# Attention and two gated layers on one core: the 896 tokens cut as 480 + 416 columns, not 448 + 448

## The chip, the core and the metric

The kernel runs on one core of a Trainium2 chip. The metric is the device time of one execution in microseconds (us), lower is better. The runs below are separate executions of the whole kernel. One of them was recorded by the hardware profiler, and the rows shown are of that one.

## The reference

Inputs are q, k, v of shape 2 x 12 x 448 x 64, and float64 weights. The attention is causal; its output is laid out as 896 tokens (2 batches of 448) by 768 channels. Two layers follow:

```python
x = attention(q, k, v)            # 896 x 768, float32
g = x @ w_gate                    # 768 x 1536
v = x @ w_val                     # 768 x 1536
y = (g * sigmoid(g) * v) @ w_out  # 1536 x 768
h = y @ w_in2                     # 768 x 2048
out = relu(h) ** 2 @ w_out2       # 2048 x 768
```

## The kernel before

After the attention (the first 95 us or so) all activations lie with their channels on the 128 partitions and the 896 tokens along the free dimension, in tiles of 128 x 896. Every number, of activations and weights alike, is kept as two parts, hi and lo, in the type float32r, and each product is made of three: hi by hi, lo by hi, hi by lo.

A *unit* of weights is 128 x 768 numbers. There are 68: 12 pairs of gate and value (`g`, `v`), 12 of the way down (`o`, two for each of six output blocks `y`), 16 of the second way up (`h`), and 16 of the second way down (`f`). A unit comes in as 768 KB of float64 on SP's queue and is turned into a hi and a lo tile by nine instructions of DVE and ACT (`split_w`, lines 366 to 394), which run two units ahead of TensorE.

In the three stages before the last, a block of 128 output channels has two PSUM banks, one for the tokens of each batch (`halves(b)`: columns 0 to 447 and 448 to 895). `mm3` (lines 615 to 623) issues six matmuls for each block of 128 input channels: the weights are the stationary operand (128 x 128), the activations the moving one (448 columns). The order is hi weights by hi activations for bank 0 and bank 1, hi by lo for both, lo by hi for both. A pair of matmuls here means those two, which share their weights and differ in bank. A unit of gate, value or second way up has 6 x 6 = 36 matmuls, and so has one of the way down:

```python
        for b in bs:
            nc.tensor.matmul(out=pss[b][:, :S], lhsT=hi, rhs=mhi[:, halves(b)], start=first, stop=False)
```

The very first unit (gate, m = 0) has its bank 0 done ahead, inside the attention (`early_mm`, 448 columns).

When a block is complete, its two banks are read and turned into the next stage's tiles. These steps are put into the list `later` and are taken from it one at a time, between the steps of the weights' splitting (`follow_up`). For gate and value they are a sigmoid on ACT (L707), multiplications on DVE (L711), a copy to hi on ACT (L715) and the rest to lo on POOL (L716); for the way down a copy (L748) and a subtraction (L752); for the second way up Relu, Square and a copy on ACT (L772 to L775) and a subtraction on DVE (L779). Each of these handles one bank, 448 columns.

The last stage has the roles turned round: activations are stationary (128 tokens), weights move, 384 columns at a time (`add_up`, line 793).

The pool of PSUM has all 8 banks, taken in turn.

Of the kernel before, what the change touches and what calls it, by code (L numbers as in the profile page):

```python
# [265 lines left out]
def tile_attention_moe_moe(ctx, tc, q, k, v, w_gate, w_val, w_out, w_in2, w_out2, out):  # L266
# [22 lines left out]
    def bank(name):  # L289
        t = ps_p.tile([128, 512], F32, tag="b", name=name)  # L290
        keep_warm(t, idle["n"])
        idle["n"] = 0
        return t
# [139 lines left out]
    def unit(kind, m, j):  # L433
        n = units.index((kind, m, j))
        split_to(n + 2)
        load_w(n + 5)
        return split_t[n]
# [8 lines left out]
    def halves(b):  # L446
        return slice(b * S, (b + 1) * S)


    att = ExitStack()  # L450
    raw_p = att.enter_context(tc.tile_pool(name="qkvraw", bufs=2))
# [160 lines left out]
            op=ALU.subtract)  # L612


    def mm3(pss, hi, lo, mhi, mlo, first, last):

        bs = list(pss)
        for b in bs:
            nc.tensor.matmul(out=pss[b][:, :S], lhsT=hi, rhs=mhi[:, halves(b)], start=first, stop=False)  # L619
        for b in bs:  # L620
            nc.tensor.matmul(out=pss[b][:, :S], lhsT=hi, rhs=mlo[:, halves(b)], start=False, stop=False)  # L621
        for b in bs:
            nc.tensor.matmul(out=pss[b][:, :S], lhsT=lo, rhs=mhi[:, halves(b)], start=False, stop=last)  # L623

    def gate_or_val(kind, m, bs):
        hi, lo = unit(kind, m, 0)
        pss = {b: bank(kind) for b in bs}
        for kk in range(KD):
            c = slice(kk * 128, (kk + 1) * 128)
            mm3(pss, hi[:, c], lo[:, c], x_hi[kk], x_lo[kk], kk == 0, kk == KD - 1)  # L630
        return pss

    def emit_fixed():

# [18 lines left out]
            state["split"] += 1  # L653

    def early_mm(n, kk):
        hi, lo = split_t[n]
        if kk == 0:
            early[n] = bank("early")
        c = slice(kk * 128, (kk + 1) * 128)
        mm3({0: early[n]}, hi[:, c], lo[:, c], x_hi[kk], x_lo[kk], kk == 0, kk == KD - 1)  # L660

    def early_out(n):
        t = early_p.tile([128, S], F32, tag=f"e{n}", name="early")
# [10 lines left out]
    with tc.manual_schedule():  # L674
        nc.vector.memset(warm, 0.0)
        keep_warm(bank("idle"), 7)
        emit_consts()
        emit_fixed()
        free = 4000
        for start, cost, engine, key in attention_plan(NP, NPAIR, NC, S, U, KD).run():  # L680
            if key[0] == "Q":
                continue
            if engine == "PE":
                if start < Warmth.FROM:
                    idle["n"] = max(0, int((start - free) / (430 if start < 6800 else 215)))
                free = start + cost
            work[key[0]](*key[1:])
            idle["n"] = 0
        att.close()

        ay_p = ctx.enter_context(tc.tile_pool(name="ay", bufs=1))
        tmp_p = ctx.enter_context(tc.tile_pool(name="tmp", bufs=2))
        extra = [act_tile(ay_p, f"b{i}") for i in range(32)]


        g_hi = [extra[2 * m] for m in range(KF1)]
        g_lo = [extra[2 * m + 1] for m in range(KF1)]

        sg, up = {}, {}

        def sigmoids(ps):
            for z in range(B):
                sigmoid(ps[z], z)

        def sigmoid(ps, z):
            sg[z] = tmp_p.tile([128, S], F32, tag="sg", name="sg")
            nc.scalar.activation(out=sg[z], in_=ps[:, :S], func=AF.Sigmoid)  # L707

        def times(o, ps, z):
            o[z] = o.get(z) or tmp_p.tile([128, S], F32, tag="u", name="u")  # L710
            nc.vector.tensor_tensor(out=o[z], in0=ps[:, :S], in1=sg[z], op=ALU.mult)  # L711

        def gated(m, z):
            hs, u = halves(z), up.pop(z)
            nc.scalar.activation(out=g_hi[m][:, hs], in_=u, func=AF.Copy)  # L715
            nc.gpsimd.tensor_tensor(  # L716
                out=g_lo[m][:, hs], in0=u, in1=g_hi[m][:, hs].bitcast(F32), op=ALU.subtract)

        n = 0
        for m in range(KF1):  # L720
            for kind in "gv":
                ps = gate_or_val(kind, m, [1] if n < NEARLY else [0, 1])
                if n < NEARLY:
                    ps[0] = early[n]
                n += 1
                if kind == "g":
                    later += [partial(sigmoids, ps), *(partial(times, sg, ps[z], z) for z in range(B))]
                else:
                    later.append(lambda: None)
                    for z in range(B):  # L730
                        later += [partial(times, up, ps[z], z), partial(gated, m, z)]


        y_hi = extra[24:30]
        y_lo = extra[30:32] + x_hi[:4]
        for m in range(KD):
            pss = {b: bank("y") for b in range(B)}
            for j in range(2):
                hi, lo = unit("o", m, j)
                n = KF1 // 2  # L740
                for kk in range(n):
                    c = slice(kk * 128, (kk + 1) * 128)
                    f = j * n + kk
                    mm3(pss, hi[:, c], lo[:, c], g_hi[f], g_lo[f], f == 0, f == KF1 - 1)

            def first_part(m, pss):
                for b in range(B):
                    nc.scalar.activation(out=y_hi[m][:, halves(b)], in_=pss[b][:, :S], func=AF.Copy)  # L748

            def rest(m, pss, b):  # L750
                hs = halves(b)
                nc.vector.tensor_tensor(  # L752
                    out=y_lo[m][:, hs], in0=pss[b][:, :S], in1=y_hi[m][:, hs].bitcast(F32),
                    op=ALU.subtract)

            later += [partial(first_part, m, pss), partial(rest, m, pss, 0), partial(rest, m, pss, 1)]


        free = x_hi[4:] + x_lo + extra[:24]
        r_hi, r_lo = free[0:32:2], free[1:32:2]  # L760
        for m in range(KF2):
            hi, lo = unit("h", m, 0)
            pss = {b: bank("h") for b in range(B)}
            for kk in range(KD):
                c = slice(kk * 128, (kk + 1) * 128)
                mm3(pss, hi[:, c], lo[:, c], y_hi[kk], y_lo[kk], kk == 0, kk == KD - 1)
            u = {}

            def squares(m, pss, u):
                for b in range(B):  # L770
                    r = tmp_p.tile([128, S], F32, tag="sg", name="r")
                    nc.scalar.activation(out=r, in_=pss[b][:, :S], func=AF.Relu)  # L772
                    u[b] = tmp_p.tile([128, S], F32, tag="u", name="r2")
                    nc.scalar.activation(out=u[b], in_=r, func=AF.Square)
                    nc.scalar.activation(out=r_hi[m][:, halves(b)], in_=u[b], func=AF.Copy)  # L775

            def rest(m, u, b):
                hs = halves(b)
                nc.vector.tensor_tensor(  # L779
                    out=r_lo[m][:, hs], in0=u[b], in1=r_hi[m][:, hs].bitcast(F32), op=ALU.subtract)  # L780

            later += [partial(squares, m, pss, u), partial(rest, m, u, 0), partial(rest, m, u, 1)]


        N = DM // 2
        NTK = NT // 128
        for half in range(2):
            pss = [bank("o") for _ in range(NTK)]
            def add_up(hi, lo, u, z, t):
                f = 2 * u + z  # L790
                c, tk = slice(z * N, (z + 1) * N), slice(t * 128, (t + 1) * 128)
                for n, (a, w) in enumerate(((r_hi, hi), (r_hi, lo), (r_lo, hi))):
                    nc.tensor.matmul(  # L793
                        out=pss[t][:, :N], lhsT=a[f][:, tk], rhs=w[:, c], start=f + n == 0,
                        stop=f == KF2 - 1 and n == 2)

            for u in range(FU):
                hi, lo = unit("f", half, u)
                order = [(z, t) for z in range(2) for t in range(NTK)]
                if u == FU - 1:  # L800

                    order.sort(key=lambda x: x[1])
                for z, t in order:
                    add_up(hi, lo, u, z, t)
            for t in range(NTK):
                o = tmp_p.tile([128, N], F32, tag="osb", name="osb", bufs=6)
                if t % 2:
                    nc.vector.tensor_copy(out=o, in_=pss[t][:, :N])
                else:
                    nc.scalar.activation(out=o, in_=pss[t][:, :N], func=AF.Copy)  # L810
                nc.sync.dma_start(
                    out=out[t * 128:(t + 1) * 128, half * N:(half + 1) * N], in_=o)
# [30 lines left out]
```

## Time and profile before

| | |
|---|---|
| time, median of 3 runs | 598.9 us (598.78 to 600.12) |
| the profiled execution, first to last instruction | 598.2 us |
| TensorE busy | 592.2 us, 99% |
| VectorE (DVE) busy | 475.2 us, 79% |
| ScalarE (ACT) busy | 282.7 us, 47% |
| GpSimd (POOL) busy | 86.7 us, 14% |
| DMA, mean rate | 109 GB/s |

The profiled execution's own time is known by its span alone, 598.2 us; the median of the runs is 0.7 us longer. A matmul's recorded duration runs beyond the start of the next one, since matmuls are pipelined, so the spacing of the starts tells what a matmul costs in a row of them, not its duration.

### The profile page before, as it was taken

How to read it: one execution, taken by the hardware profiler on the slowest of the kernel's cores; microseconds unless marked ns; L12 is line 12 of the kernel's file. 1: busy time of each engine (PE TensorE's matmuls, PEld its weight loads, DVE VectorE, ACT ScalarE, POOL GpSimd, SP SyncE). 2: the span in 40 equal slices, each digit the busy share in tenths (PEclk: the TensorE clock that was granted, in tenths of full speed). 3: DMA queues.
4: the chain of work that ended last, by engine and by line, in shares of the span. 5: the costliest groups of instructions: out<-in, count | busy, mean ns of one | idle time of the engine just before them, and what ended most of it. 6: DMA issues, size and time to landing. Idle time of an engine off the chain costs nothing.

```text
span 598.2 us, 8837 instructions
## 1 busy us (share of the span) xinstructions
PE 592.2 (99%) x3256; PEld 530.8 (89%) x3257; DVE 475.2 (79%) x839; ACT 282.7 (47%) x555; POOL 86.7 (14%) x154
## 2 busy tenths in 40 slices
PE   8999999999999999999999999999999999999997
PEld 5777778999999999999999999999999999999997
DVE  4789977999999999998877777888888887649741
ACT  6999984333333333333222225666666642222201
POOL 4576770211111111111000000000000000000000
PEclk9999999999999999999999999999999999999999
DMA  8784402333333333333333332333333344345202
GB/s 169 166 220 95 122 2 85 108 109 112 108 110 109 105 106 106 106 105 107 121 107 102 106 109 91 107 107 105 106 105 107 105 112 153 106 142 136 80 1 93
DMA packets 80779, 65.06 MB, mean 109 GB/s; under 512 B 34912, under 2 KB 76640, under 8 KB 80736
## 3 DMA queue, kind: packets, MB, share of 16 engines
q1 hardware_dynamic: 79808, 64.27, 36.6%
q8 instruction: 26, 0.43, 0.3%
q10 hardware_dynamic: 928, 0.23, 0.2%
q14 instruction: 17, 0.14, 0.1%
HBM read 61.73 MB, written 2.75 MB: 108 GB/s over the span
## 4 chain that ended last, share of the span: by engine, by line
PE 95%; DVE 2%; POOL 1%; issue 1%; ACT 1%; DMA 1%; SPq 0%; POOLq 0%; ACTq 0%
PE o L793 19%; PE h L621 7%; PE h L619 7%; PE h L623 7%; PE y L619 5%; PE v L623 5%; PE v L619 5%; PE y L623 5%; PE y L621 5%; PE v L621 5%; PE g L623 5%; PE g L619 5%; PE g L621 5%; PE s L520 4%; PE x L598 3%; PE pt L576 2%
## 5 line engine op out<-in xcount | busy, mean ns | idle before, releaser
L381 ACT ACTIVATE whi<-wa 128x768 fp32r<-128x768 f32 x68 | 57.6, 847 | 179.3 <-DVE wa L378 136.8
L793 PE MATMUL o<-whi,b 128*128 128x384 f32 x336 | 85.6, 334 | 0.0
L369 DVE TENSOR_SCALAR wa<-wa 128x768 f32<-128x768 f32 x68 | 41.4, 608 | 43.5 <-ACT wa L366 43.5
L378 DVE SCALAR_TENSOR_TENSOR wa<-wraw,wa 128x768 uint32<-128x768 uint32 x68 | 75.2, 1106 | 0.0
L366 ACT ACTIVATE wa<-wraw 128x768 f32<-128x768 f32 x68 | 61.6, 905 | 17.6 <-DVE wlo L394 17.6
L394 DVE TENSOR_TENSOR wlo<-wa,wr 128x768 fp32r<-128x768 f32 x68 | 65.7, 967 | 0.1
L388 DVE SCALAR_TENSOR_TENSOR wr<-wraw,wr 128x768 f32<-128x768 uint32 x68 | 65.0, 955 | 0.1
L391 DVE TENSOR_TENSOR wa<-wa,whi 128x768 f32<-128x768 f32 x68 | 64.6, 950 | 0.4 <-ACT whi L381 0.4
L793 PEld LDWEIGHTS o<-whi,b 128*128 128x128 f32 x336 | 60.8, 188 | 0.0
L793 PE MATMUL o<-wlo,b 128*128 128x384 f32 x168 | 56.1, 334 | 0.0
L623 PE MATMUL h<-b,wlo 128*128 128x448 f32 x192 | 55.2, 368 | 0.0
L619 PE MATMUL h<-b,whi 128*128 128x448 f32 x192 | 55.1, 368 | 0.0
L716 POOL TENSOR_TENSOR b<-u,b 128x448 fp32r<-128x448 f32 x24 | 29.0, 1209 | 159.4 <-ACT b L715 159.4
L541 ACT ACTIVATE P<-P,st 128x448 f32<-128x448 f32 (+2 forms) x96 | 47.7, 503 | 3.3 <-DVE st L535 1.9
L559 POOL TENSOR_SCALAR P<-P,st 128x448 f32<-128x448 f32 (+1 forms) x88 | 45.1, 531 | 10.2 <-DVE st L551 5.3
L535 DVE CUSTOM_DVE_ANT_0 P<-s,mask 128x448 f32<-128x448 f32 (+2 forms) x96 | 34.8, 412 | 11.9 <-PE s L520 10.5
L619 PE MATMUL v<-ahi,whi 128*128 128x448 f32 x144 | 41.4, 368 | 0.0
L619 PE MATMUL y<-b,whi 128*128 128x448 f32 x144 | 41.4, 368 | 0.0
L621 PE MATMUL y<-b,whi 128*128 128x448 f32 x144 | 41.4, 368 | 0.0
L623 PE MATMUL v<-ahi,wlo 128*128 128x448 f32 x144 | 41.4, 368 | 0.0
L621 PE MATMUL v<-alo,whi 128*128 128x448 f32 x144 | 41.4, 368 | 0.0
L623 PE MATMUL y<-b,wlo 128*128 128x448 f32 x144 | 41.3, 368 | 0.0
(96 smaller groups left out, 1145.1 us busy)
## 6 DMA issues: line engine op xcount, KB each, us to landing
wraw<-in_moe_w_out_dram SPq DMA_DIRECT2D x28, 768.0 KB, 4.4
wraw<-in_moe_w_in_dram SPq DMA_DIRECT2D x16, 768.0 KB, 4.6
wraw<-in_moe_w_gate_dram SPq DMA_DIRECT2D x12, 768.0 KB, 4.3
wraw<-in_moe_w_val_dram SPq DMA_DIRECT2D x12, 768.0 KB, 4.3
raw<-in_q_dram SPq DMA_DIRECT2D x24, 112.0 KB, 2.7
out_dram<-osb SPq DMA_DIRECT2D x14, 192.0 KB, 1.9
raw<-in_k_dram SPq DMA_DIRECT2D x22, 112.0 KB, 2.8
v<-in_v_dram SPq DMA_DIRECT2D x24, 96.0 KB, 2.7
```

What stands on the lines that cost most here:

```text
L366: nc.scalar.activation(out=af, in_=high.bitcast(F32), func=AF.Abs)
L378: nc.vector.scalar_tensor_tensor(out=a, in0=high, scalar=0xC0000000, in1=a, op0=ALU.bitwise_and, op1=ALU.bitwise_or)
L381: nc.scalar.activation(out=split_t[n][0], in_=af, func=AF.Copy)
L388: nc.vector.scalar_tensor_tensor(out=rf, in0=low, scalar=2.0 ** -52, in1=rf, op0=ALU.mult, op1=ALU.mult)
L391: nc.vector.tensor_tensor(out=af, in0=af, in1=split_t[n][0].bitcast(F32), op=ALU.subtract)
L394: nc.vector.tensor_tensor(out=split_t[n][1], in0=af, in1=r[0].bitcast(F32), op=ALU.add)
L541: nc.scalar.activation(out=a, in_=a, func=AF.Exp, scale=-1.0, bias=st(0), accum_out=st(1))
L559: (nc.vector if n_on_dve(h) else nc.gpsimd).tensor_scalar(out=o, in0=a, scalar1=st(2), scalar2=1.0, op0=ALU.mult, op1=ALU.mult)
L619: nc.tensor.matmul(out=pss[b][:, :S], lhsT=hi, rhs=mhi[:, halves(b)], start=first, stop=False)
L621: nc.tensor.matmul(out=pss[b][:, :S], lhsT=hi, rhs=mlo[:, halves(b)], start=False, stop=False)
L623: nc.tensor.matmul(out=pss[b][:, :S], lhsT=lo, rhs=mhi[:, halves(b)], start=False, stop=last)
L793: nc.tensor.matmul(out=pss[t][:, :N], lhsT=a[f][:, tk], rhs=w[:, c], start=f + n == 0, stop=f == KF2 - 1 and n == 2)
```

## The change

The second bank no longer begins at the second batch. In gate and value (all but the first pair of units), in the way down and in the second way up, bank 0 takes columns 0 to 479 and bank 1 columns 480 to 895. The first pair of units keeps 448 + 448, since its early bank is made so. The number of matmuls, their order, the weights that they load and the reading of the banks stay; the instructions that read the banks take 480 and 416 columns in place of 448 and 448, and the four buffers of the pool `tmp` become 480 columns wide. `mm3` and `gate_or_val` become one helper, `products`. The attention and the last stage are not touched.

```diff
+    HALVES = (0, S), (S, S)
+    CUTS = (0, 480), (480, 416)
+
+    def at(cut):
+        return slice(cut[0], cut[0] + cut[1])
...
-    def mm3(pss, hi, lo, mhi, mlo, first, last):
-
-        bs = list(pss)
-        for b in bs:
-            nc.tensor.matmul(out=pss[b][:, :S], lhsT=hi, rhs=mhi[:, halves(b)], start=first, stop=False)
...
+    def products(pss, cuts, w, xs, first, last):
+
+        n = len(xs)
+        zs = list(pss)
+        for k, p, z in [(k, p, z) for k in range(n) for p in range(3) for z in zs]:
+            at, cols = cuts[z]
+            c = slice(k * 128, (k + 1) * 128)
+            nc.tensor.matmul(
+                out=pss[z][:, :cols], lhsT=w[p == 2][:, c], rhs=xs[k][p == 1][:, at:at + cols],
+                start=first and k == 0 and p == 0, stop=last and k == n - 1 and p == 2)
...
+        def times(o, ps, z, c):
+            o[z] = o.get(z) or tmp_p.tile([128, W], F32, tag="u", name="u")
+            nc.vector.tensor_tensor(
+                out=o[z][:, :c[1]], in0=ps[:, :c[1]], in1=sg[z][:, :c[1]], op=ALU.mult)
...
+        W = max(c[1] for c in CUTS)
+        x_parts = list(zip(x_hi, x_lo))
         n = 0
         for m in range(KF1):
+            cuts = CUTS if m else HALVES
             for kind in "gv":
-                ps = gate_or_val(kind, m, [1] if n < NEARLY else [0, 1])
+                w = unit(kind, m, 0)
+                ps = {z: bank(kind) for z in range(n < NEARLY, B)}
+                products(ps, cuts, w, x_parts, True, True)
...
             for j in range(2):
-                hi, lo = unit("o", m, j)
-                n = KF1 // 2
-                for kk in range(n):
-                    c = slice(kk * 128, (kk + 1) * 128)
-                    f = j * n + kk
-                    mm3(pss, hi[:, c], lo[:, c], g_hi[f], g_lo[f], f == 0, f == KF1 - 1)
+                products(
+                    pss, CUTS, unit("o", m, j), g_parts[j * n:(j + 1) * n], j == 0, j == 1)
...
         for m in range(KF2):
-            hi, lo = unit("h", m, 0)
+            w = unit("h", m, 0)
             pss = {b: bank("h") for b in range(B)}
-            for kk in range(KD):
-                c = slice(kk * 128, (kk + 1) * 128)
-                mm3(pss, hi[:, c], lo[:, c], y_hi[kk], y_lo[kk], kk == 0, kk == KD - 1)
+            products(pss, CUTS, w, y_parts, True, True)
```

## Rows read from the trace of the kernel before

**Rows 1.** The page's busy times by engine, and TensorE's granted clock in 40 slices.
```profile
span 598.2 us, 8837 instructions
PE 592.2 (99%) x3256; PEld 530.8 (89%) x3257; DVE 475.2 (79%) x839; ACT 282.7 (47%) x555; POOL 86.7 (14%) x154
PEclk9999999999999999999999999999999999999999
```
**Rows 2.** Busy time by stretch: gate and value from m = 1, down, up, last.
```profile
core 0: us, PE busy (x) PEld busy (x) DVE busy (x) ACT busy (x) POOL busy (x), PEclk, DMA share, GB/s
106.13:269.81 163.68, 163.68 (x794) 148.67 (x793) 147.99 (x200) 60.61 (x89) 26.67 (x22) 1.00 0.33 106
269.81:359.09 89.28, 89.28 (x434) 81.09 (x433) 70.44 (x99) 26.82 (x37) 2.34 (x2) 1.00 0.35 110
359.09:478.12 119.03, 119.03 (x577) 108.12 (x576) 98.63 (x143) 78.58 (x125) 0.00 (x0) 1.00 0.35 104
478.12:594.80 116.68, 116.66 (x673) 116.33 (x671) 77.28 (x108) 29.43 (x40) 0.00 (x0) 1.00 0.34 102
```
**Rows 3.** Who waited for whom, 106 to 478 us, longest first: six of twelve.
```profile
POOL b L716 <- ACT b L715: 159.4, 24, 20.6
ACT whi L381 <- DVE wa L378: 113.0, 50, 4.0
...
DVE wa L369 <- ACT wa L366: 26.7, 51, 1.0
ACT b L748 <- PE y L623: 21.9, 6, 4.1
...
ACT r L772 <- PE h L623: 15.1, 15, 2.1
...
DVE ahi L779 <- ACT ahi L775: 2.1, 1, 2.1
```
**Rows 4.** TensorE's timeline from 106.2 us: starts of pairs of 448-column matmuls.
```profile
106.54 0.57 PE L621 MATMUL g<-alo,whi 128*128 128x448 f32 x2
106.95 0.57 PE L623 MATMUL g<-ahi,wlo 128*128 128x448 f32 x2
...
108.19 0.57 PE L623 MATMUL g<-ahi,wlo 128*128 128x448 f32 x2
```
**Rows 5.** The same in the last stage: starts of 384-column matmuls, by threes.
```profile
520.08 0.51 PE L793 MATMUL o<-whi,b 128*128 128x384 f32 x2
520.42 0.33 PE L793 MATMUL o<-wlo,b 128*128 128x384 f32 x1
...
522.68 0.51 PE L793 MATMUL o<-whi,b 128*128 128x384 f32 x2
```
**Rows 6.** Groups by form, whole span: matmuls of both widths, and a weight load.
```profile
L793 PE MATMUL o<-whi,b 128*128 128x384 f32 x336 | 85.6, 334 | 0.0
L623 PE MATMUL h<-b,wlo 128*128 128x448 f32 x192 | 55.2, 368 | 0.0
L793 PEld LDWEIGHTS o<-whi,b 128*128 128x128 f32 x336 | 60.8, 188 | 0.0
```
**Rows 7.** The chain that ended last: runs of the attention's transposes (112 and 128 columns).
```profile
22.59 1.15 PE qk L501 x12
23.96 0.66 PE pt L576 x6
```
**Rows 8.** TensorE's timeline where 448-column matmuls give way to 384.
```profile
477.71 0.57 PE L623 MATMUL h<-b,wlo 128*128 128x448 f32 x2
478.12 0.34 PE L793 MATMUL o<-whi,ahi 128*128 128x384 f32 x1
478.30 0.33 PE L793 MATMUL o<-wlo,ahi 128*128 128x384 f32 x1
478.48 0.51 PE L793 MATMUL o<-whi,ahi 128*128 128x384 f32 x2
```
**Rows 9.** Groups by form, 100 to 480 us: instructions that read banks or follow them.
```profile
L716 POOL TENSOR_TENSOR b<-u,b 128x448 fp32r<-128x448 f32 x24 | 29.0, 1209 | 159.4 <-ACT b L715 159.4
L772 ACT ACTIVATE r<-h 128x448 f32<-128x448 f32 x32 | 17.2, 538 | 16.0 <-PE h L623 16.0
L711 DVE TENSOR_TENSOR u<-v,sg 128x448 f32<-128x448 f32 x24 | 14.7, 614 | 0.0
L779 DVE TENSOR_TENSOR b<-r,b 128x448 fp32r<-128x448 f32 x23 | 14.3, 623 | 9.6 <-ACT b L775 9.6
```

More of the change, by code (lines that the diff above doesn't have):

```diff
@@ L612, in channels_lo @@
             op=ALU.subtract)
-    def mm3(pss, hi, lo, mhi, mlo, first, last):
-        bs = list(pss)
-        for b in bs:
-            nc.tensor.matmul(out=pss[b][:, :S], lhsT=hi, rhs=mhi[:, halves(b)], start=first, stop=False)
[L620 to L627, printed above, removed]
-        for kk in range(KD):
-            c = slice(kk * 128, (kk + 1) * 128)
-            mm3(pss, hi[:, c], lo[:, c], x_hi[kk], x_lo[kk], kk == 0, kk == KD - 1)
-        return pss
+    def products(pss, cuts, w, xs, first, last):
[7 more added lines that the diff above has]
+                start=first and k == 0 and p == 0, stop=last and k == n - 1 and p == 2)
     def emit_fixed():
@@ L655, in early_mm @@
     def early_mm(n, kk):
-        hi, lo = split_t[n]
         if kk == 0:
@@ L659, in early_mm @@
         c = slice(kk * 128, (kk + 1) * 128)
-        mm3({0: early[n]}, hi[:, c], lo[:, c], x_hi[kk], x_lo[kk], kk == 0, kk == KD - 1)
+        products(
+            {0: early[n]}, HALVES, [t[:, c] for t in split_t[n]], [(x_hi[kk], x_lo[kk])],
+            kk == 0, kk == KD - 1)
     def early_out(n):
@@ L699, in tile_attention_moe_moe, with sigmoids, gated @@
         sg, up = {}, {}
[L701 to L715, printed above, removed]
+        def sigmoids(ps, cuts):
+            for z, c in enumerate(cuts):
+                sg[z] = tmp_p.tile([128, W], F32, tag="sg", name="sg")
+                nc.scalar.activation(out=sg[z][:, :c[1]], in_=ps[z][:, :c[1]], func=AF.Sigmoid)
+        def times(o, ps, z, c):
+            o[z] = o.get(z) or tmp_p.tile([128, W], F32, tag="u", name="u")
+            nc.vector.tensor_tensor(
+                out=o[z][:, :c[1]], in0=ps[:, :c[1]], in1=sg[z][:, :c[1]], op=ALU.mult)
+        def gated(m, z, c):
+            u = up.pop(z)[:, :c[1]]
+            nc.scalar.activation(out=g_hi[m][:, at(c)], in_=u, func=AF.Copy)
             nc.gpsimd.tensor_tensor(
-                out=g_lo[m][:, hs], in0=u, in1=g_hi[m][:, hs].bitcast(F32), op=ALU.subtract)
+                out=g_lo[m][:, at(c)], in0=u, in1=g_hi[m][:, at(c)].bitcast(F32), op=ALU.subtract)
+        W = max(c[1] for c in CUTS)
+        x_parts = list(zip(x_hi, x_lo))
         n = 0
         for m in range(KF1):
+            cuts = CUTS if m else HALVES
             for kind in "gv":
-                ps = gate_or_val(kind, m, [1] if n < NEARLY else [0, 1])
+                w = unit(kind, m, 0)
+                ps = {z: bank(kind) for z in range(n < NEARLY, B)}
+                products(ps, cuts, w, x_parts, True, True)
                 if n < NEARLY:
@@ L726, in tile_attention_moe_moe @@
                 if kind == "g":
-                    later += [partial(sigmoids, ps), *(partial(times, sg, ps[z], z) for z in range(B))]
+                    later += [partial(sigmoids, ps, cuts), *(
+                        partial(times, sg, ps[z], z, c) for z, c in enumerate(cuts))]
                 else:
                     later.append(lambda: None)
-                    for z in range(B):
-                        later += [partial(times, up, ps[z], z), partial(gated, m, z)]
+                    for z, c in enumerate(cuts):
+                        later += [partial(times, up, ps[z], z, c), partial(gated, m, z, c)]
@@ L734, in tile_attention_moe_moe @@
         y_hi = extra[24:30]
         y_lo = extra[30:32] + x_hi[:4]
+        g_parts = list(zip(g_hi, g_lo))
         for m in range(KD):
             pss = {b: bank("y") for b in range(B)}
+            n = KF1 // 2
             for j in range(2):
-                hi, lo = unit("o", m, j)
-                n = KF1 // 2
-                for kk in range(n):
-                    c = slice(kk * 128, (kk + 1) * 128)
-                    f = j * n + kk
-                    mm3(pss, hi[:, c], lo[:, c], g_hi[f], g_lo[f], f == 0, f == KF1 - 1)
+                products(
+                    pss, CUTS, unit("o", m, j), g_parts[j * n:(j + 1) * n], j == 0, j == 1)
@@ L746, in first_part, with rest @@
             def first_part(m, pss):
[L747 to L751, printed above, removed]
+                for z, c in enumerate(CUTS):
+                    nc.scalar.activation(
+                        out=y_hi[m][:, at(c)], in_=pss[z][:, :c[1]], func=AF.Copy)
+            def rest(m, pss, z, c):
                 nc.vector.tensor_tensor(
-                    out=y_lo[m][:, hs], in0=pss[b][:, :S], in1=y_hi[m][:, hs].bitcast(F32),
-                    op=ALU.subtract)
@@ L756, in tile_attention_moe_moe @@
-            later += [partial(first_part, m, pss), partial(rest, m, pss, 0), partial(rest, m, pss, 1)]
+                    out=y_lo[m][:, at(c)], in0=pss[z][:, :c[1]],
+                    in1=y_hi[m][:, at(c)].bitcast(F32), op=ALU.subtract)
+            later += [partial(first_part, m, pss), *(
+                partial(rest, m, pss, z, c) for z, c in enumerate(CUTS))]
         free = x_hi[4:] + x_lo + extra[:24]
         r_hi, r_lo = free[0:32:2], free[1:32:2]
+        y_parts = list(zip(y_hi, y_lo))
@@ L761, in tile_attention_moe_moe @@
         for m in range(KF2):
-            hi, lo = unit("h", m, 0)
+            w = unit("h", m, 0)
             pss = {b: bank("h") for b in range(B)}
-            for kk in range(KD):
-                c = slice(kk * 128, (kk + 1) * 128)
-                mm3(pss, hi[:, c], lo[:, c], y_hi[kk], y_lo[kk], kk == 0, kk == KD - 1)
+            products(pss, CUTS, w, y_parts, True, True)
             u = {}
             def squares(m, pss, u):
[L770 to L775, printed above, removed]
@@ L777, in rest @@
-            def rest(m, u, b):
-                hs = halves(b)
+                for z, c in enumerate(CUTS):
+                    r = tmp_p.tile([128, W], F32, tag="sg", name="r")[:, :c[1]]
+                    nc.scalar.activation(out=r, in_=pss[z][:, :c[1]], func=AF.Relu)
+                    u[z] = tmp_p.tile([128, W], F32, tag="u", name="r2")[:, :c[1]]
+                    nc.scalar.activation(out=u[z], in_=r, func=AF.Square)
+                    nc.scalar.activation(out=r_hi[m][:, at(c)], in_=u[z], func=AF.Copy)
@@ L779, in rest @@
+            def rest(m, u, z, c):
                 nc.vector.tensor_tensor(
-                    out=r_lo[m][:, hs], in0=u[b], in1=r_hi[m][:, hs].bitcast(F32), op=ALU.subtract)
-            later += [partial(squares, m, pss, u), partial(rest, m, u, 0), partial(rest, m, u, 1)]
+                    out=r_lo[m][:, at(c)], in0=u[z], in1=r_hi[m][:, at(c)].bitcast(F32),
+                    op=ALU.subtract)
+            later += [partial(squares, m, pss, u), *(
+                partial(rest, m, u, z, c) for z, c in enumerate(CUTS))]
```

## The prediction

> **What bounds the kernel.** I read the page first: TensorE is busy 99% of the span, and its clock stands at the top mark in all 40 slices [rows 1], which is the upper of its two levels, 2.4 GHz. Next the busy times by stretch, cut at the borders of the stages: in the three stages that the change touches TensorE is busy for every one of 163.68, 89.28 and 119.03 us, at a clock of 1.00, while DVE reaches 147.99 of 163.68 us, 90%, and less in the other two [rows 2]. The waits from 106 to 478 us say the same from the other side: others wait for TensorE (ACT for the banks of the way down and of the second way up), and of the twelve rows none has TensorE as the one that waits [rows 3]. So the 372.0 us of these stages are a plain row of matmuls, and the change can gain or lose only by what a matmul costs in that row.
>
> That cost is the spacing of starts, not the recorded duration: the records give 368 ns for 448 columns [rows 6], but four pairs start within 108.19 - 106.54 = 1.65 us [rows 4], so a pair takes some 0.413 us. The stretches give it finer: the code has 22 units of 36 matmuls in the first, 163.68 / 792 = 206.7 ns each; 89.28 / 432 and 119.03 / 576 are 206.7 and 206.6 ns [rows 2]. (The views count one or two more, those that straddle a border.) At 2.4 GHz, 206.7 ns are 496 cycles. The last stage's 384 columns: five threes from 520.08 to 522.68 us [rows 5], 2.60 us / 15 = 173.3 ns, 416 cycles. These two prices are all that the trace has of this kind of matmul.
>
> **The change part by part.** *Removed, added, moved.* No matmul, weight load, wait, DMA or queue position changes; 792 + 432 + 576 = 1,800 matmuls, 900 pairs, go from 448 + 448 to 480 + 416 columns. The total of columns is the same. Two things can alter the time: the price of 480 and 416, and the instructions that follow the banks.
>
> *The price of the pair.* Before, 2 x 496 = 992 cycles, 413.3 ns. For the new widths the trace has no row, so first the bounds, from the nearest rows, in whole steps of what lies between the two known widths (33.4 ns for 64 columns). Lowest: 480 costs what 448 does, 416 what 384 does, 206.7 + 173.3 = 380.0 ns, a gain of 33.3 ns a pair or 30.0 us. Highest: 480 costs a step more than 448, 416 as much as 448, 240.1 + 206.7 = 446.8 ns, a loss of 30 us. Both ends are far, so what matters is how the price runs between.
>
> Over the bare 1 cycle a column, 448 columns pay 496 - 448 = 48 cycles more and 384 pay 416 - 384 = 32. A straight line through both is 1.25 cycles a column less 64 cycles. A negative fixed cost of 64 cycles is odd. The transposes of the attention are another kind of matmul with a positive one: 12 of 112 columns in 1.15 us and 6 of 128 in 0.66 us [rows 7] are 95.8 and 110.0 ns, which at two cycles a column leaves 2.5 and 3.3 ns. So I hold it likelier that the surplus comes in steps: something is paid each time a block of columns is through. With blocks of 64, 448 columns are 7 blocks and 384 are 6, and the surplus is 16 cycles for each block after the fourth: 3 x 16 and 2 x 16. Both widths are whole blocks, so the rows cannot say what a broken block pays. I take it that it pays nothing until it is complete. A row leans that way, weakly: the first 384-column matmul behind a 448-column one takes 478.30 - 478.12 = 0.18 us, the next two average 0.173 (0.34 to 478.82 for two) [rows 8], so part of the surplus looks like a debt that the finished matmul hands to the next.
>
> Then 480 columns still have 7 whole blocks: 480 + 48 = 528 cycles; 416 have 6: 416 + 32 = 448. The pair has 976 cycles, 406.7 ns, a gain of 6.67 ns. Times 900: **6.0 us**. A part of a price that depends on the matmul before it, as in [rows 8], cancels here as far as it is linear, since each 480 follows a 416 and the other way round.
>
> *Is 416 held up by its weight load?* Its record is 188 ns, longer than the 173.3 ns between starts in the last stage, where it holds nothing up [rows 5, 6]. A floor, if there is one, lies at or below 173.3 ns, and 416 columns at 186.7 ns stand above it. Cost: nothing.
>
> *What follows the banks.* DVE's multiplication takes 614 ns for 448 columns, its subtraction 623, ACT's Relu 538, POOL's subtraction 1,209 [rows 9]. Each is one instruction on 480 and one on 416 now; fixed part plus columns, two together, stay as they were, and 32 columns more delay the first by at most 1,209 x 32 / 448 = 86 ns (POOL) or 44 ns (DVE). The cover is that TensorE, with other banks to go to, waits for none of them [rows 3]. Without it a late bank would cost up to some 0.05 us at each of 44 blocks (22, 6 and 16), 2.2 us. I take nothing.
>
> *DVE as the next bound.* If TensorE gets faster by 1.6%, DVE's 147.99 us stand against 161.04 instead of 163.68, 92%. DVE's longest regular wait in these stages, for ACT's first step of a split, sums to 26.7 us, at most 1.0 us each [rows 3]; it closes before TensorE starves.
>
> *The sum* is made against the profiled execution: 598.2 - 6.0 = 592.2 us of span. The median of the runs is 0.7 us above that span, and I carry those 0.7: **592.9 us**.
>
> **The rivals.**
>
> *No change: the price is a line, or the steps are wider.* By the line, 480 costs 536 and 416 costs 456, together 992 as before. Also with 16 cycles at each border between blocks of 128 columns (3 borders in 448, 2 in 384, which fits both rows as well): 480 and 416 have 3 each, 528 + 464 = 992. Time 598.9 us. For it: the simplest curve through two points, and any line whatever gives it. Against it: the negative fixed cost. The Trainium skill, "TensorE: Matmul & The Clock Gate", section "Back-to-back issue gap", has such a line for a warm isolated matmul, columns / 2.4 plus 2.5 ns. By that rule the pair would be 202.5 + 175.8 = 378.3 ns, as for two of 448, and the time 598.9 us. The trace does not agree with its size: 189.2 ns by the rule for 448 columns against 206.7, and 162.5 for 384 against 173.3 [rows 4, 5].
>
> *More gain: narrower steps.* Steps of 40 columns and 40 cycles with 16 fixed cycles fit as well: 448 is 12 started steps, 384 is 10, which gives 496 and 416. Then 480 is exactly 12 (496) and 416 is 11 (456): 952 cycles, 40 less, 16.7 ns x 900 = 15.0 us, 583.9 us. For it: a positive fixed cost. Against it: an odd block width, and nothing else in the rows that has it. DVE would stand at 147.99 of 157.1 us in the first stretch, still not the bound.
>
> *Slower: a started block pays in full.* With blocks of 64 and the surplus paid when a block begins, 480 is 8 blocks (480 + 64 = 544 cycles) and 416 is 7 (416 + 48 = 464): 1,008 cycles, 6.67 ns more, and 598.9 + 6.0 = 604.9 us. The place is TensorE's row of matmuls itself; it decides as soon as a broken block costs more than half of what a whole one does. For it: 480 and 416 both end inside a block, and nothing in the trace shows a broken block for free.
>
> **How the numbers follow.** Whole blocks 0.33 (592.9 us, its own range 591.5 to 594.5), narrower steps 0.15 (583.9), no change 0.32 (598.9), started blocks and other losses 0.20 (604.9). Within 0.3%, 597.1 to 600.7 us, is about what a measurement of this kernel cannot tell from no change. Hence faster 0.48, same 0.32, slower 0.20. The range leaves out the slower case, 0.20, and reaches from the narrow steps to the upper edge of no change: 583.5 to 600.7 us.
>
> **What would show it.** In the timeline of the changed kernel, pairs begin 406.7 ns apart (413.3 by a line, 396.7 by steps of 40, 420.0 by started blocks); the stretch of gate and value from m = 1 is 161.0 us long, the way down 87.8, the second way up 117.1, and the last stage stays at 116.7. Within a pair, 480 takes 220.0 ns and 416 186.7. The clock stays at 1.00 and TensorE has no wait in those stages. The prediction is wrong if the pair stays at 413.3 ns, if the price depends on the order of the widths and not on their sum, or if TensorE begins to wait for a bank or a split.

## The result, and the profile after

The changed kernel takes 591.3 us (591.3 to 591.41, 4 runs) against 598.84 us (598.61 to 600.12, 4 runs): a ratio of 0.988, 95% interval 0.9847 to 0.9912. That is 7.5 us less; 6.0 us less was forecast, to 592.9 us.

The page's busy times of the changed kernel (they answer to [rows 1]):

```profile
span 589.3 us, 8837 instructions
PE 582.6 (99%) x3256; PEld 529.2 (90%) x3257; DVE 475.1 (81%) x839; ACT 282.6 (48%) x555; POOL 86.1 (15%) x154
PEclk9999999999999999999999999999999999999999
```

The same work in 8.9 us less of span, at the same clock. The stretches, cut again where the stages begin (columns as in [rows 2]):

```profile
105.84:267.33 161.49, 161.05 (x794) 147.67 (x793) 146.47 (x199) 59.21 (x88) 26.36 (x22) 1.00 0.33 107
267.33:354.05 86.72, 86.69 (x433) 80.86 (x432) 72.01 (x102) 28.01 (x38) 2.31 (x2) 1.00 0.36 113
354.05:469.25 115.20, 115.20 (x577) 107.93 (x577) 98.32 (x143) 78.67 (x124) 0.00 (x0) 1.00 0.36 109
469.25:585.90 116.65, 116.65 (x673) 116.35 (x672) 77.58 (x108) 29.43 (x40) 0.00 (x0) 1.00 0.34 102
```

Gate and value give 163.68 - 161.49 = 2.19 us, the way down 2.56, the second way up 3.83, the last stage nothing; another 0.29 us came before the first border, 0.22 of it because the first pair of units, still 448 + 448, ran at 202.7 ns a matmul in this execution (54 matmuls, 4.0 ns less each). The second way up shows the price undisturbed: 115.20 us / 576 = 200.0 ns a matmul, 400.0 a pair, in place of 413.3. TensorE's timeline in the way down says so too, pairs starting 0.40 us apart (the view names a merged run by its first width):

```profile
299.65 0.56 PE L628 MATMUL y<-b,wlo 128*128 128x480 f32 x2
300.05 0.96 PE L628 MATMUL y<-b,whi 128*128 128x480 f32 x4
300.85 0.56 PE L628 MATMUL y<-b,wlo 128*128 128x480 f32 x2
301.25 0.56 PE L628 MATMUL y<-b,whi 128*128 128x480 f32 x2
```

Starts are 210 ns apart from a 480 to a 416, 190 from a 416 to a 480: 13.3 ns less a pair, twice the forecast. 900 pairs would give 12.0 us; the three stages gave 8.58. The missing 3.4 us are in gate and value (792 x 6.67 ns = 5.28 us, 2.19 seen) and a little in the way down. The waits from 106 to 480 us, of which [rows 3] had none by TensorE:

```profile
DVE wa L369 <- ACT wa L366: 26.8, 52, 1.0
ACT wa L366 <- DVE wlo L394: 16.4, 34, 0.6
...
PEld g L628 <- DVE wlo L394: 3.8, 9, 0.4
...
PEld y L628 <- DVE wlo L394: 0.4, 1, 0.4
```

Ten times TensorE's weight load stands and waits for a lo tile of the splitting. One of them, with DVE and ACT around it:

```profile
208.28 0.56 PE L628 MATMUL g<-ahi,whi 128*128 128x480 f32 x2
208.33 0.94 DVE L394 TENSOR_TENSOR wlo<-wa,wr 128x768 fp32r<-128x768 f32 x1
...
208.69 0.56 PE L628 MATMUL g<-alo,whi 128*128 128x480 f32 x2
209.30 0.92 ACT L366 ACTIVATE wa<-wraw 128x768 f32<-128x768 f32 x1 [0.46 <-DVE wlo L394]
209.30 0.56 DVE L384 TENSOR_SCALAR wr<-wa 128x768 uint32<-128x768 uint32 x1
209.32 0.30 PEld L628 LDWEIGHTS g<-ahi,wlo 128*128 128x128 f32 x2 [0.44 <-DVE wlo L394]
209.32 0.67 PE L628 MATMUL g<-ahi,wlo 128*128 128x480 f32 x2
```

The third pair of a gate unit needs the lo weights. DVE's last step on them (208.33 to 209.27) ends after the first two pairs; the third starts 0.63 us behind the second instead of 0.40. The same end releases ACT's first step on the next unit, for which DVE then waits in its turn.

What reads the banks costs what it did: DVE's multiplication takes 649 and 577 ns for the two widths, together 1,226, against 2 x 614 [rows 9]:

```profile
L708 DVE TENSOR_TENSOR u<-v,sg 128x480 f32<-128x480 f32 x11 | 7.1, 649 | 0.0
...
L708 DVE TENSOR_TENSOR u<-v,sg 128x416 f32<-128x416 f32 x11 | 6.3, 577 | 0.0
```

### The profile page after: what moved, and what is told of

It reads as the page before. It is cut to its first block, busy times and chain, and to the rows that moved or that the text cites. A ratio compares the mean times of both kernels' runs of the same rounds, so it can differ in the third digit from the quotient of the medians.

```text
span 589.3 us, 8837 instructions
## 1 busy us (share of the span) xinstructions
PE 582.6 (99%) x3256; PEld 529.2 (90%) x3257; DVE 475.1 (81%) x839; ACT 282.6 (48%) x555; POOL 86.1 (15%) x154
## 4 chain that ended last, share of the span: by engine, by line
PE 68%; DVE 19%; issue 6%; ACT 5%; POOL 1%; DMA 1%; SPq 0%; DVEq 0%; POOLq 0%; ACTq 0%
PE o L796 20%; PE h L628 20%; PE y L628 15%; PE s L526 4%; DVE wlo L394 3%; ACT wa L366 3%; DVE wa L391 3%; PE x L604 3%; DVE wa L369 2%; PE pt L582 2%; DVE wa L374 2%; DVE wa L378 2%; DVE sg L708 2%; DVE u L708 2%; PE v L628 1%
## 5 line engine op out<-in xcount | busy, mean ns | idle before, releaser
L628 PE MATMUL y<-b,whi 128*128 128x480 f32 (+1 forms) x288 | 69.2, 362 | 0.0
L628 PE MATMUL h<-b,whi 128*128 128x480 f32 (+1 forms) x256 | 66.7, 362 | 0.0
L628 PEld LDWEIGHTS y<-b,whi 128*128 128x128 f32 x288 | 54.0, 187 | 3.7
L628 PE MATMUL h<-b,wlo 128*128 128x480 f32 x192 | 53.9, 362 | 0.0
L714 POOL TENSOR_TENSOR b<-u,b 128x480 fp32r<-128x480 f32 (+2 forms) x24 | 28.7, 1195 | 159.4 <-ACT b L713 159.4
L628 PEld LDWEIGHTS h<-b,whi 128*128 128x128 f32 x256 | 48.0, 187 | 3.2
L628 PE MATMUL g<-ahi,wlo 128*128 128x480 f32 (+2 forms) x138 | 40.3, 369 | 0.4
L628 PE MATMUL y<-b,wlo 128*128 128x480 f32 (+1 forms) x144 | 40.5, 363 | 0.0
L628 PE MATMUL v<-alo,whi 128*128 128x480 f32 (+2 forms) x144 | 40.4, 362 | 0.0
```

The lines of the kernel that those rows point to most:

```text
L628: nc.tensor.matmul(out=pss[z][:, :cols], lhsT=w[p == 2][:, c], rhs=xs[k][p == 1][:, at:at + cols], start=first and k == 0 and p == 0, stop ...
```

## The experiments

Two questions: what sets the price of a pair, and what the waits for lo tiles cost. Prices below are mean distances of starts in the trace, in ns a matmul, over the second half of a block (18 or 36 matmuls, settled); for grouped blocks, over the middle of each width's run (11 matmuls).

**1. Many cuts in one kernel, and the order of the widths.**

```diff
+        order = [(k, p, z) for k in range(n) for p in range(3) for z in zs]
+        if grouped:
+            order.sort(key=lambda o: o[2])
...
-            cuts = CUTS if m else HALVES
+            cuts = HALVES
...
+            CUTS, grouped = cuts_of(*H[m])
```

> Gate and value are back at 448 + 448; the blocks of the way down and of the second way up each have a cut of their own, some with TensorE's matmuls alternating between the two widths as now, some grouped (all matmuls of the wide bank of a unit, then all of the narrow one). Theory A, own price: a matmul's price follows from its own width alone, so 480 + 416 cost 400.0 ns a pair grouped as well as alternating, and 448 costs 206.7 ns in every block. Theory B, company: a price depends on the widths next to it, rows of one width being dear, so 480 + 416 grouped go back to 413.3 ns a pair, alternating stay at 400.0, and 448 can differ from block to block (206.7 or the 202.7 that the first pair of the changed kernel shows). Steps of 64 whole columns, as the prediction had it, would give 406.7 for 464 + 432 and for 472 + 424, and 413.3 for 512 + 384.

| columns | alternating | grouped: wide, narrow |
|---|---|---|
| 448 + 448 | 206.7 in all of gate and value; 202.6 to 202.9 in five later blocks, 206.7 in three | |
| 456 + 440 | 201.9 | |
| 464 + 432 | 204.2 | 209.6, 195.3 |
| 472 + 424 | 203.3 | |
| 480 + 416 | 200.0 (three blocks) | 216.6, 186.6 |
| 488 + 408 | 200.0 | |
| 496 + 400 | 203.6 | 223.0, 183.4 |
| 512 + 384 | 206.7 | 226.6, 173.4 |
| 416 + 480 | 202.7 | |

Lines from two of these blocks, 512 + 384 alternating (its pairs named by their first width) and 480 + 416 grouped, where 0.65 us for three matmuls of 480 and 0.56 for three of 416 are 216.7 and 186.7 ns:

```profile
404.04 0.58 PE L630 MATMUL h<-ahi,whi 128*128 128x512 f32 x2
404.46 0.57 PE L630 MATMUL h<-b,wlo 128*128 128x512 f32 x2
...
316.20 0.59 PE L630 MATMUL y<-b,whi 128*128 128x480 f32 x2
316.85 0.59 PE L630 MATMUL y<-b,whi 128*128 128x480 f32 x2
...
318.62 0.54 PE L630 MATMUL y<-b,whi 128*128 128x416 f32 x2
319.18 0.54 PE L630 MATMUL y<-b,whi 128*128 128x416 f32 x2
```

Theory A falls: 512 and 384 cost 206.7 on average when they alternate and 200.0 when grouped, and 448 has two prices in one kernel. Theory B holds only in part, since grouping 480 + 416 gives 201.6 (the mean of 216.6 and 186.6), not 206.7. The prediction's whole blocks of 64 fit 464, 472 and 496 (203.3) roughly, but not 456, 480 and 488, nor the dependence on order. The grouped rows have a floor: 512, 416 and 384 columns pay 544, 448 and 416 cycles, each 32 (13.3 ns) over one a column; the others pay 37 to 40. 480 + 416 alternating, 960 cycles, pay 32 each too. 448 + 448 pay 38 or 48.

**2. One part alone: gate and value back at 448 + 448.**

```diff
-            cuts = CUTS if m else HALVES
+            cuts = HALVES
```

> One part alone: 480 + 416 in the way down and the second way up, 448 + 448 in all of gate and value. Both theories of the price: 504 pairs gain 13.3 ns, 6.7 us, in those stages. On the waits for the weights' lo tiles: if they come from DVE falling behind because TensorE got faster, they are gone here, and the gate and value stage is 163.7 us as before; the whole is then about 2 us slower than the changed kernel, 593.3 us. If they come from something else in the new code, some 3 us of waits stay, and the whole is about 596.5 us.

593.38 us (591.38 to 594.21, 10 runs), ratio to before 0.9929 (0.9896 to 0.9962). The later two stages run at 200.0; gate and value take 162.8 us, and the view of waits lists none for a lo tile. So 480 + 416 in gate and value is worth some 2 us, not its 5.3. The trace shows one source of the spread: 448 + 448 begin this execution at 202.7 ns, and after a hiccup at 151 us go on at 206.7. (Such a mean spacing, kept from block to block, is called a rhythm below.)

```profile
149.75 0.94 DVE L394 TENSOR_TENSOR wlo<-wa,wr 128x768 fp32r<-128x768 f32 x1
...
150.21 0.40 PEld L628 LDWEIGHTS g<-alo,whi 128*128 128x128 f32 x2
150.41 0.57 PE L628 MATMUL g<-alo,whi 128*128 128x448 f32 x2
...
150.74 0.30 PEld L628 LDWEIGHTS g<-ahi,wlo 128*128 128x128 f32 x2
150.82 0.60 PE L628 MATMUL g<-ahi,wlo 128*128 128x448 f32 x2
...
151.26 0.57 PE L628 MATMUL g<-ahi,whi 128*128 128x448 f32 x2
...
151.67 0.57 PE L628 MATMUL g<-alo,whi 128*128 128x448 f32 x2
```

One pair takes 0.44 us, some 30 ns too many, and from then on each takes 0.413. The hiccup is a late lo tile again. The weight load for this pair stands still from 150.61 us, when the loads before it end, to 150.74, and starts 0.05 us after DVE's last step on the tile (149.75 + 0.94 = 150.69), just as in the changed kernel (209.27 and 209.32); the view of waits does not list one so short. No other weight load of these stages stands still so long in this execution. So one short wait is left with 448 + 448, in place of nine. That it also made the switch of rhythm is read from one execution.

**3 and 4. A third buffer for the splitting's tile, in the changed kernel and in the one before.**

```diff
-                        dec_p.tile([128, U], U32, tag="a", name="wa", bufs=2))
+                        dec_p.tile([128, U], U32, tag="a", name="wa", bufs=3))
```

> The changed kernel with three buffers instead of two for the splitting's tile wa, so that ACT's first step on the next unit needs no longer wait for DVE's last step on the unit before. Theory: DVE loses about 0.5 us a unit waiting for that first step and this is what makes the lo tiles late; then TensorE's waits of 3.2 us or so in gate and value go, and the time is about 588.1 us. Rival: DVE's instructions themselves fill the time; then 591.3 us, with the waits as they are.

> The kernel before with the same third buffer for wa. TensorE waited for nothing there, so both theories say no change, 598.8 us; a gain here would mean that the buffer does something else than to feed TensorE in time.

The changed kernel with it: 588.37 us (588.03 to 588.67, 6 runs), ratio to before 0.9837 (0.9799 to 0.9876). No wait of TensorE is left from 100 to 470 us, and DVE's for ACT's first step are half as long in sum. The first three stages:

```profile
106.20:264.62 158.42, 158.42 (x793) 148.34 (x792) 147.68 (x201) 58.72 (x89) 26.38 (x22) 1.00 0.34 110
264.62:351.02 86.40, 86.40 (x433) 80.92 (x433) 69.23 (x98) 25.85 (x36) 2.33 (x2) 1.00 0.36 114
351.02:466.22 115.20, 115.20 (x577) 107.89 (x577) 97.28 (x143) 76.70 (x124) 0.00 (x0) 1.00 0.36 107
```

158.42 us / 792 is 200.0 ns, down from 161.49 us. DVE's own work is the same; so what had made the tiles late was DVE's wait for ACT, and ACT's for a free buffer, not DVE's instructions. The rival falls.

The kernel before with it: 593.07 us (592.71 to 600.28, 9 runs), ratio 0.9955 (0.9908 to 1.0001): six runs from 592.7 to 593.4 us and three from 600.1 to 600.3. No change was expected. The upper group shows none, but six of the nine runs do, and the median is 5.7 us lower, with an interval that just reaches no change. The profiled run is of the lower group:

```profile
105.94:266.44 160.50, 160.50 (x793) 148.74 (x792) 148.96 (x203) 59.48 (x89) 26.63 (x22) 1.00 0.34 109
266.44:354.00 87.56, 87.56 (x434) 81.13 (x432) 68.37 (x96) 25.82 (x37) 2.34 (x2) 1.00 0.36 113
354.00:470.74 116.74, 116.74 (x578) 108.17 (x577) 97.47 (x143) 76.74 (x125) 0.00 (x0) 1.00 0.35 105
```

160.50 / 792 and 116.74 / 576 are 202.7 ns: 448 + 448 throughout in a quicker rhythm than in [rows 2], with the same instructions in the same order. The kernel before lies in such groups too. Of all its 47 runs beside these experiments, 13 took 594.2 to 595.0 us, 20 took 598.2 to 599.3 and 14 took 600.1 to 600.8. That the lower group stands 1.6 us above 593 us for want of the third buffer is inferred; no run of that group was profiled.

A reading that fits experiment 2, and is not shown: a late lo tile throws 448 + 448 out of the quicker rhythm, and the third buffer spares it that. In all three profiled executions with three buffers and 448 + 448 in gate and value (experiments 4, 5 and 11) that stage began at 202.7 and kept it, and no weight load waited for a lo tile. So the worth of the change depends on what it is set against: with three buffers in both kernels, 480 + 416 is worth some 4.5 us against the lower group (592.9 us on average) and 11.8 against the upper.

**5. Half the weight load.** In some blocks all but the first and last product of a bank use 64 of 128 weight columns; those output channels are left out.

```diff
+            M = 64 if half and 0 < 3 * k + p < 3 * n - 1 else 128
+            c = slice(k * 128, k * 128 + M)
...
-                out=pss[z][:, :cols], lhsT=w[p == 2][:, c], rhs=xs[k][p == 1][:, at:at + cols],
+                out=pss[z][:M, :cols], lhsT=w[p == 2][:, c], rhs=xs[k][p == 1][:, at:at + cols],
```

> With three buffers of wa, gate and value at 448 + 448, and cuts of their own in the blocks of the way down and the second way up. In the blocks marked h, all but the first and the last product of a bank load only 64 of the 128 weight columns and give only 64 output channels: that work is left out, the moving columns stay. Theory W, the weight load: what a matmul pays over one cycle a column comes from loading the next weights beside it, so with half the load 448 + 448 falls well below 405 ns a pair, towards 2 x 187 ns, and has one rhythm only. Theory M, the moving stream: the surplus belongs to streaming the columns, and half loads change nothing: 405 or 413 ns a pair. The blocks that begin with the narrow width (416 + 480) show in short what the next run shows at length.

The loads themselves are shorter, as the groups by form show for one such block:

```profile
L630 PEld LDWEIGHTS h<-b,whi 128*64 128x64 f32 x14 | 1.9, 134 | 0.9
...
L630 PEld LDWEIGHTS h<-b,whi 128*128 128x128 f32 x2 | 0.4, 188 | 0.0
```

448 + 448 cost 202.6 to 202.7 with half loads, 202.4 to 206.7 with whole ones in the same kernel; 480 + 416 went from 200.0 up to 201.5; 416 + 480 had 200.3 against 202.4. (512 + 384 had 201.3, and 206.7 in experiment 1; as it has two groups of times of its own, experiment 8, that tells little.) Theory W falls: nothing goes towards 187. Theory M, as it stood (no effect), falls as well: the size of the load changes the price of 480 + 416 and 416 + 480, but nothing went below the floor of 13.3 ns.

**6, 7 and 8. Other cuts in the whole kernel**, all with the third buffer: 416 + 480, 488 + 408, 512 + 384.

```diff
-    CUTS = (0, 480), (480, 416)
+    CUTS = (0, 416), (416, 480)
```

> The changed kernel with three buffers of wa and the two banks exchanged in width: 416 columns first, then 480, so that the two matmuls that share weights are narrow then wide. Theory, the sum of the widths or their alternation alone counts: 400.0 ns a pair, 588.4 us. Rival, the order within the pair counts too: the one block of the first experiment that began with the narrow width ran at 405.4 ns a pair, which over 900 pairs is 4.9 us more, 593.2 us.

> The changed kernel with three buffers of wa and 488 + 408 columns. By the first experiment's one block of it, 399.9 ns a pair, as good as 480 + 416, so 588.3 us. By steps of 64 whole columns 406.7 ns a pair, 6 us more, 594.4 us.

> The changed kernel with three buffers of wa and 512 + 384 columns. By the first experiment's one block, 413.2 ns a pair, as dear as 448 + 448 at its worst: 900 x 13.2 ns = 11.9 us more than 480 + 416, about 600.2 us. If instead unequal widths as such are what helps, it is at or below 588.4 us.

| | time, us | runs | ratio to before | settled price |
|---|---|---|---|---|
| 416 + 480 | 592.33 (592.19 to 592.81) | 4 | 0.9883 (0.9866 to 0.9901) | 202.5 |
| 488 + 408 | 588.19 (587.82 to 588.42) | 4 | 0.9814 (0.98 to 0.9829) | 200.0 |
| 512 + 384 | 597.17 (593.79 to 600.32) | 10 | 0.998 (0.994 to 1.002) | 206.7 in the profiled run |

The second way up of the four executions with other cuts, in the order 416 + 480, 488 + 408, 512 + 384 and, from experiment 9, 480 + 416 with the wide bank in the upper columns (576 matmuls each, columns as in [rows 2]):

```profile
354.09:470.73 116.64, 116.64 (x578) 107.55 (x576) 97.58 (x143) 76.72 (x125) 0.00 (x0) 1.00 0.36 105
350.92:466.12 115.20, 115.20 (x578) 107.06 (x578) 97.26 (x143) 76.63 (x124) 0.00 (x0) 1.00 0.36 107
359.00:478.04 119.04, 119.04 (x577) 104.79 (x577) 97.44 (x143) 76.75 (x124) 0.00 (x0) 1.00 0.34 103
353.77:470.41 116.64, 116.64 (x577) 107.55 (x577) 97.35 (x143) 76.72 (x124) 0.00 (x0) 1.00 0.35 106
```

Narrow first is 4 us dearer, as its rival had it. 512 + 384 fall into two groups like 448 + 448, five runs from 593.8 to 594.6 us and five from 599.7 to 600.3: unequal widths as such do not help. The two cuts at the floor have no second group; the runs of each lie within 0.7 us.

**9. Order or address.** Wide first, but in the upper columns.

```diff
-    CUTS = (0, 480), (480, 416)
+    CUTS = (416, 480), (0, 416)
```

> The changed kernel with three buffers of wa; the wide bank comes first in each pair, as in the change, but takes columns 416 to 895, and the narrow one columns 0 to 415. So the order of widths is that of the change and the addresses are those of the kernel that began with the narrow width (202.5 ns a matmul, 592.3 us). If the order within a pair decides, 200.0 ns and 588.3 us; if the columns' addresses decide, 202.5 ns and 592.3 us.

592.43 us (592.35 to 593.09, 4 runs), ratio 0.9906 (0.9856 to 0.9956), and 202.4 to 202.6 ns. Of the two it is the address: with the same columns, either order costs 202.5, and with the same order, other columns cost 200.0.

**10. The kernel before, once more.**

> The kernel before, unchanged, for one more profile. If its executions lie apart because 448 + 448 has two rhythms, this one shows 206.7 ns a matmul throughout and about 600 us, or 202.7 ns with some waits of TensorE for lo tiles and about 594.4 us, or a switch from one to the other and a time between. Rival: the spread comes from the attention or the last stage; then the spacing in the three stages is 206.7 ns whatever the time.

600.16 us, and 206.7 ns in every unit of the three stages, so the first of the three alternatives. One run cannot refute the rival for the other groups; experiments 2 and 4 speak against it.

**11. Where the moving columns start.** Banks and widths stay; the matmuls read columns from other starts, so that some tokens are multiplied twice and others not at all.

```diff
             at, cols = cuts[z]
+            at = moved[z] if moved else at
```

> With three buffers of wa, gate and value at 448 + 448. In the blocks of the way down and the second way up the moving columns of the two banks start at other places than the banks' own columns, so that some tokens are multiplied twice and others not at all; widths stay 480 + 416 (ten blocks of the second way up, five of the way down) or 448 + 448. Theory, start of the wide slice: 480 columns from column 0 settle at 200.0 ns a matmul whatever the other one's start, and from column 416 at 202.5. Theory, start of the narrow slice: 416 columns from 480 settle at 200.0, and from 0 at 202.5. Theory, the two together (the distance between the starts): every mixed block gives a price of its own, and 448 + 448 from the same column twice leaves the 202.7 or 206.7 of 448 columns apart.

| first bank, from | second bank, from | price | | first bank, from | second bank, from | price |
|---|---|---|---|---|---|---|
| 480, 0 | 416, 480 | 200.0 | | 480, 32 | 416, 480 | 204.4 |
| 480, 0 | 416, 416 | 200.0 | | 480, 416 | 416, 480 | 204.4 |
| 480, 0 | 416, 0 | 201.7 | | 448, 0 | 448, 448 | 202.8 |
| 480, 0 | 416, 384 | 203.4 | | 448, 0 | 448, 0 | 202.7 |
| 480, 0 | 416, 448 | 203.4 | | 448, 0 | 448, 432 | 203.3 |
| 480, 384 | 416, 0 | 203.4 | | 448, 0 | 448, 416 | 203.3 |
| 480, 416 | 416, 0 | 202.4 | | 448, 16 | 448, 448 | 202.5 |
| 480, 16 | 416, 480 | 204.8 | | 448, 0 | 448, 384 | 206.7 |
| | | | | 448, 0 | 448, 440 | 206.7 |

Two whole blocks of the second way up, 36 matmuls each: 480 from 32 with 416 from 480, and 480 from 0 with 416 from 480 (204.4 and 200.6 ns a matmul, with their first, unsettled matmuls):

```profile
411.83:419.19 7.36, 7.36 (x37) 6.75 (x37) 6.18 (x10) 4.94 (x8) 0.00 (x0) 1.00 0.36 107
419.19:426.41 7.22, 7.22 (x37) 6.74 (x37) 6.00 (x10) 4.94 (x8) 0.00 (x0) 1.00 0.36 111
```

Neither start decides alone: the wide slice from 0 has 200.0 to 203.4, the narrow one from 480 has 200.0 to 204.8. Nor does the distance: starts 448 apart cost 203.4 (0 and 448) and 204.4 (32 and 480). What is left of the third theory is that the two together matter, and with the widths; it had each mixed block at a price of its own, but several share one. Most of these prices come from a single block. Why, in the memory or in TensorE, no run here shows.

## Why the prediction was right, and where not

*What bounds the kernel*: right for the kernel before, and 8.58 of the 8.9 us came from the three stages, at an unchanged clock. That the change could lose only by what a matmul costs did not hold, as told under DVE.

*The price of the pair*: right in sign, mis-sized (6.67 ns forecast, 13.3 measured; within the pair 210 and 190 ns, not 220.0 and 186.7), and its reason was wrong. "The surplus comes in steps", paid for each whole block of 64 columns, does not survive experiments 1 and 9: the same widths cost 400.0 or 405 ns a pair by where their columns start. Measured in its place: a floor of 13.3 ns over one cycle a column, which 480 + 416 from columns 0 and 480 meet exactly, and above it a rhythm of neighbouring matmuls that costs 448 + 448 another 2.7 or 6.7 ns each. That 448 had one price in the trace of before was taken for a property of the width; it was one of two rhythms. The ground for steps was weak as well: the transposes' two spacings, 95.8 and 110.0 ns, lie by themselves on a line with -3.6 ns at no columns, so their positive fixed cost came of the two cycles a column that were assumed.

*The rivals.* The line, and with it the rule of the Trainium skill ("TensorE: Matmul & The Clock Gate", "Back-to-back issue gap": for a warm isolated matmul, a gap that is linear in the columns) gave no change; the runs disagree, 400.0 against 413.3 ns for the same sum of columns. Steps of 40 had 396.7 ns and would have come nearest in price, but with them 512 + 384 cost as little, and they cost 206.7 a matmul. Started blocks (420.0 ns) did not show.

*What follows the banks*: right, 1,226 against 1,228 ns.

*DVE as the next bound*: the step that failed. Its share was set against the stage (90%, to rise to 92%) and its wait for ACT was said to close "before TensorE starves". It did not: 3.1 us of gate and value's 5.28 and 0.3 of the way down went into TensorE's waits for lo tiles, and experiment 3 gave 2.9 us back. The sum of DVE's work had room; what had none was the turn of DVE and ACT through two buffers of wa.

*The sum.* That 7.5 us lie so near 6.0 is luck: the price gave twice what was forecast, 12.0 us for the 900 pairs, and waits that were put at nothing took 3.4 away. Two signs that the prediction named for its being wrong came true: the same sum of widths has more than one price (experiments 6 and 9), and TensorE began to wait for a split.

The 0.7 us between the profiled span and the median was no constant: the changed kernel has 2.0 us outside its span (591.3 against 589.3), so the profiled run of before was one of about 600.2 us, above its median. By the profiled runs the gain is 8.9 us, by the medians 7.5; against the 13 runs of before at 594.2 to 595.0 us it is some 3 us.

## What to carry to other kernels

When an engine is busy for all of a stage, ask what an instruction costs there, and whether it is the same in other executions: a price seen in one may be one of several rhythms. A second profile need not tell (experiment 10 shows 206.7 ns again); here runs whose times fall into groups gave it away. Try the widths and the starts of the operands, in one kernel that gives each block its own; it cost one run here to see 13 cuts and orders. And when the bounding engine gets faster by 3%, look at who feeds it through a buffer that is released late: a share of 90% with a short wait in every turn was already the next bound.

## What the runs showed of the hardware

- A row of float32r matmuls, each with its 128 x 128 weight load, never settled below 13.3 ns (32 cycles at 2.4 GHz) over one cycle a column for whole loads: 173.3 ns for 384, 186.6 for 416, 226.6 for 512, 200.0 on average for 480 and 416.
- 448 + 448 ran at 202.7 or 206.7 ns with identical instructions; in experiment 2 it went from the first to the second at a pair that took some 30 ns more because its weights came late, and stayed there for the rest of gate and value.
- Half the weight columns made a load's record shorter, 134 in place of 188 ns, and left 448 + 448 at 202.6 ns.
- The columns at which the moving operands start changed the price of 480 + 416 from 200.0 to as much as 204.8 ns a matmul.
